# A fused attention and gated-FFN backward kernel: second edge unit turned by DMA in two of four column groups

## The chip, the cores and the metric

The kernel runs on one core of a Trainium2 chip. Its engines work side by side, each through its own instructions in order: TensorE (PE in the profile, its weight loads PEld), VectorE (DVE), ScalarE (ACT), GpSimd (POOL) and SyncE (SP), whose queue issues most DMAs. They wait for one another through semaphores. The metric is the device time of one execution in microseconds (us); lower is better.

## The reference, cut to what matters

The reference is a forward function and its gradients. Input `x` is 2048 rows of 512. Branch A is attention with 32 heads of 16 over a causal window of 256 rows; branch B is a gated FFN with 1376 columns. A sigmoid gate mixes them:

```python
qkv = (x @ wqkv).reshape(B, S, 3, H, Dh)          # transposed to q, k, v per head
scores = jnp.einsum("bhqd,bhkd->bhqk", q, k) * (Dh ** -0.5)
mask = (i - j >= 0) & (i - j < 256)
p = softmax(where(mask, scores, -1e9))
a = einsum("bhqk,bhkd->bhqd", p, v) @ wo
b = (gate * (gate > 0) * up) @ W_down             # gate = x @ W_gate, up = x @ W_up
out = g * a + (1 - g) * b                         # g = sigmoid((x * gate_w).sum(-1))
```

It returns `out` and the gradients of `A_x`, `A_wqkv`, `A_wo`, `B_W_gate`, `B_W_up`, `B_W_down` and `gate_w`, in bf16.

## The kernel before

The program has three stages. The first computes the FFN's products and gradients (lines 205 to 469). The second, which the change touches, computes attention and its gradients (lines 471 to 1089). The third forms the output and the gradient of `x` (lines 1091 to 1180).

**Blocks, units and turns of the loop.** Rows are cut into 16 blocks of 128 (`NT`). Heads are taken in four column groups `c` of eight heads (`DC` is 4). With a window of 256, query block `qb` meets key blocks `qb`, `qb-1` and `qb-2`; the last is the edge, of which only a corner counts. A `Unit` is two heads with up to two blocks. Two units, `x` = 0 and 1, share a loop turn (`turns_`, lines 679 to 702), and share its tiles. For every pair of query blocks there are six loop turns, `k` = 0 to 5: pair turns at 0, 1, 3 and 4, and edge turns at 2 and 5. The last pair of blocks of a group has four turns; the third of them holds a diagonal block with an edge block and counts as edge. A group has 46 turns, the loop 184.

**What one loop turn does** (`while`, line 969). `products` puts the score products S of this turn's units, and the products D of the previous turn's units, on PE. `front` takes the exponential of S into a tile PP (ScalarE, line 746); `mask` zeroes what lies outside the window (GpSimd, line 756); `gradp` multiplies the previous turn's PP by its D into PP's second half (VectorE, line 763). Then every unit's PP, eight blocks of 128 by 128, is needed in two ways:

- As it is, by the sums of the rows (`rowsum`, lines 780 and 782, four small matmuls a call). A row's twelve sums close it; small operations on GpSimd over the next four turns follow. `some_sums` runs at most `quota[0]` of them in a turn, five while the loop has units.
- Turned (transposed), by `cd_piece` (lines 495 and 498), which adds up the gradients of keys and values. It may use a row three loop turns after that row closed, and runs two or three pieces a turn.

**How a unit is turned** (`flip`, line 806). If `u.dma` is set, SyncE issues a DMA transpose of the whole unit, 256 KB (line 809), in the loop turn after the unit's own, when `gradp` is done. Otherwise PE transposes the eight blocks into PSUM two loop turns after the unit's own (line 817) and `share` evicts them on VectorE or ScalarE, whichever its running estimate finds less busy. Before the change `u.dma` holds for unit `x == 0` of every turn with two blocks (but for the very first turns and the very last).

**Tiles.** PP of pair turns has four buffers, PP of edge turns (tag `PPm`) two. Turned tiles of pair units (tag `P2`, line 795) have 14 buffers; those of both edge units share a tile with tag `m`, of four.

**Background work.** Projections of the next rows and groups (`project_parts`), the weight gradients of the group before (`grad_parts`, which read `dar` rows loaded by DMA) and the rest of the FFN's gradients stand in a list `bg`, with a price each. The loop spends them evenly up to the loop turn `until`. When list and jobs are empty in the last group, `early_group` is made: its loads for the third stage (`early`, lines 870 to 873) go out one each turn.

**Third stage.** It works through eight groups of 256 rows. Each group's operands are loaded one group ahead by `load_group`, among them a DMA transpose of `dqkvo_d` (line 912).

Of the kernel before, what the change touches and what calls it, by code (L numbers as in the profile page):

```python
# [11 lines left out]
BF = mybir.dt.bfloat16  # L12
# [10 lines left out]
def kernel(  # L23
# [21 lines left out]
    P = 128  # L45
# [9 lines left out]
    NT = S // P  # L55
    DC = D // P
# [4 lines left out]
    TPG = TGW // P  # L61
# [58 lines left out]
    def wide(name):  # L120
        return wq.tile([P, 2, 2, 4, P], BF, tag="m", bufs=4, name=name)
# [5 lines left out]
    pools = {}  # L127

    def rows_tile(name):
        return st.tile([P, NT, 4, P], BF, tag="rows_st", name=name)  # L130

    if True:
        HH = HG // 2
        proj = {}
        groups = [(c, tg) for c in range(DC) for tg in range(NTG)]
# [69 lines left out]
    with ExitStack() as p1, tc.manual_schedule():  # L205
# [121 lines left out]
        for fc in range(FC):  # L327
            for tg in range(NTG):
                k = Step()
# [141 lines left out]
    if True:  # L471
        p3b = ExitStack()
        pjs["b"] = p3b.enter_context(tc.tile_pool(name="pj", bufs=2))
        wk = p3b.enter_context(tc.tile_pool(name="attw", bufs=2))
# [4 lines left out]
        P2 = {}  # L479
# [26 lines left out]
        def spill(c, t0):  # L506
            tsl = slice(t0, t0 + NT // 4)
            eng = nc.gpsimd if (c == DC - 1 and t0 >= NT // 2) else nc.sync
            eng.dma_start(dqkvo_d[t0 * P:(t0 + NT // 4) * P, c * 4 * P:(c + 1) * 4 * P].rearrange("(t p) n -> p t n", p=P),
                          sts[c][:, tsl, :, :].rearrange("p t a n -> p t (a n)"))  # L510
# [169 lines left out]
        for c in range(DC):  # L680
            def pair_of(q):
                return [(q, q), (q + 1, q)]

            def edges_of(r):
                return [(k, k - 2) for k in (r, r + 1) if 2 <= k < NT]

            for q in range(0, NT, 2):
                if q + 2 < NT:
                    its = ((pair_of(q), 0), (pair_of(q), 2), (edges_of(q + 1), 0), (pair_of(q + 1), 2), (pair_of(q + 1), 0),
                           (edges_of(q + 2), 2))  # L690
                else:
                    its = ((pair_of(q), 0), (pair_of(q), 2), ([(q + 1, q + 1), (q + 1, q - 1)], 0), ([(q + 1, q + 1)], 2))
                for k, (blocks, g) in enumerate(its):
                    two = []
                    for x in range(2):
                        u = Unit()
                        u.c, u.q, u.g, u.x, u.blocks, u.nb, u.at = c, q + k // 3, g + x, x, blocks, len(blocks), len(turns_)
                        u.edge = blocks[-1][1] == blocks[-1][0] - 2
                        u.dma = x == 0 and len(blocks) == 2 and (c > 0 or q > 0 or k >= 3) and (c < DC - 1 or q < NT - 2)
                        u.turn = u.at + (1 if u.dma else 2)  # L700
                        two.append(u)
                    turns_.append(two)
        NI = len(turns_)
# [33 lines left out]
        def flat(t, n):  # L737
            return t.rearrange("p x i r q -> p x (i r q)")[:, :, 0:n]

        def front(us):  # L740
            edge = us[0].edge
            two = wk.tile([P, 2, 2, 4, P], BF, tag="PPm" if edge else "PP", bufs=2 if edge else 4, name="PP")
            for u in us:
                u.two, u.PP = two, two[:, u.x, :, :, :]
            n = 2 * us[0].nb * P
            nc.scalar.activation(two[:].rearrange("p x a b q -> p x a (b q)")[:, :, 0, 0:n], flat(us[0].S[:], n), ACT.Exp)  # L746
# [42 lines left out]
        def place(u):  # L789
            if u.edge:  # L790
                if u.at not in wides:
                    wides[u.at] = wide("p2")
                p2 = wides[u.at][:, u.x if u.nb == 2 else 0, :, :, :]
            elif u.nb == 2 or u.x == 0:
                p2 = pools["p2"].tile([P, 2, 4, P], BF, tag="P2", bufs=14, name="p2")[:]
                wides[u.at] = p2
            else:
                p2 = wides[u.at]
            for i, (qb, kb) in enumerate(u.blocks):
                b = 2 * (i if u.nb == 2 else u.x)  # L800
                P2[(u.c, qb, kb, u.g)] = p2[:, :, b:b + 2, :]
            return p2
# [3 lines left out]
        def flip(u):  # L806
            p2 = place(u)
            if u.dma:
                nc.sync.dma_start_transpose(out=p2.rearrange("p a b q -> p (a b) q"),
                                            in_=u.PP.rearrange("p a b q -> p (a b) q"))  # L810
                return
            if u.nb == 2 or u.x == 0:
                pools["pt"] = ps.tile([P, 2, 4, P], BF, tag="tr", bufs=2, name="pt")
            pt = pools["pt"]
            for a in range(2):
                for b in range(2 * u.nb):
                    nc.tensor.transpose(pt[:, a, b if u.nb == 2 else 2 * u.x + b, :], u.PP[:, a, b, :], ident[:])  # L817
            return (lambda: share(p2, pt[:], 8 * P, True)) if u.nb == 2 or u.x == 1 else None
# [63 lines left out]
        def early_f(i):  # L882
            t = wide("f")[:].rearrange("p u a h q -> p (u a h q)").rearrange("p (k s) -> p k s", s=GT * P)
            gsl = slice(0, GT * P)
            for k0, k1, src in ((8 * i, 8 * i + 8, hT_d), (8 * i - FC, 8 * i + 8 - FC, dgT_d)):
                lo, hi = max(k0, 0), min(k1, FC)
                if lo >= hi:
                    continue
                for k in range(lo, hi):
                    S2.setdefault("f0" if src is hT_d else "f1", []).append(t[:, k - k0, :])  # L890
                full = min(hi, nfull)
                if lo < full:
                    nc.sync.dma_start(t[:, lo - k0:full - k0, :], src[lo * P:full * P, gsl].rearrange("(fc p) s -> p fc s", p=P))
                if hi > nfull:
                    nc.sync.dma_start(t[:, nfull - k0, :], src[F - P:F, gsl])
# [23 lines left out]
        with tc.manual_schedule():  # L919
# [9 lines left out]
            quota = [0]  # L929
            credit = 0.0  # L930
            until = 0
            turn = 0
# [9 lines left out]
            def insert(job):  # L942
                at = 0
                if held:
                    while bg[at][2]:
                        at += 1
                    at += 1
                bg[at:at] = job
# [20 lines left out]
            while turn < NI + 3 or ev or cdq or bg or sums:  # L969
                for e in busy:  # L970
                    busy[e] = max(0.0, busy[e] - 2.3) + (1.0 if e == "act" else 1.25)
                now = ev.pop(turn, [])
                quota[0] = 5 if turn < NI else 99
                us = turns_[turn] if turn < NI else []
                vs = turns_[turn - 1] if 1 <= turn <= NI else []
                for eng, f in now:
# [2 lines left out]
                if us and (turn == 0 or turns_[turn - 1][0].q != us[0].q):  # L979
                    c, j = us[0].c, us[0].q  # L980
                    gi = c * NTG + j // TPG
                    if j == 0:
                        sts[c] = rows_tile("rows_st")
                    if j % TPG == 0:
                        credit = 0.0
                        until = turn + (12 if j < NT - TPG else 10) - ((0 if c > 0 and j >= TPG else 1) if gi + 1 < len(groups) else 6)
                        if j == TPG and c > 0:
                            jobs = ready
                        for _ in range(((2, 1, 0, 0) if c == 0 else (0, 1, 2, 2))[j // TPG]):
                            if jobs:  # L990
                                bg += jobs.pop(0)
                        if gi + 1 < len(groups):
                            insert(project_parts(*groups[gi + 1]) + [(0.0, lambda gi=gi: late.extend(plan.get(gi + 1, [])), False)])
                            if gi + 2 == len(groups):
                                until -= 1
                    if j == 6 and c > 0:
                        for i in range(2):
                            ev.setdefault(turn + 7 + 4 * i, []).append(("dma", lambda c=c - 1, t0=NT // 2 + i * NT // 4: spill(c, t0)))
                    if j == 2 and c > 0:
                        ready = grad_parts(c - 1)  # L1000
                    if c == DC - 1 and j == NT - 2:
                        for i in range(3):
                            ev.setdefault(turn + (5, 6, 8)[i], []).append(("dma", lambda i=i: early_f(i)))
# [4 lines left out]
                if us:  # L1008
                    front(us)
                    mask(us)  # L1010
# [200 lines left out]
```

## Time and profile before

| | |
|---|---|
| three runs | 894.53, 888.96, 895.00 us; median 894.53 |
| profiled execution | 890.63 us, of which the span of its instructions is 888.9 |
| granted TensorE clock, mean | 0.994 |
| attention loop, first exponentials of the groups | 242.3, 349.7, 466.3, 580.5 us; last one at 692.2 |
| PE busy in the span | 848.5 us (95%) |
| VectorE, GpSimd, ScalarE busy | 503.5, 488.5, 387.2 us |
| PE transposes of line 817 | 1512, 115.3 us busy |
| DMA turns of line 809 | 171, median 4.4 us from issue to landing |
| DMA | 161.95 MB; 134, 159, 163 and 192 GB/s in the four groups |

A busy time is the time in which an engine had an instruction in work; on PE the instructions overlap and their ends are modelled, so the mean of one is longer than the step from one to the next. A row of a group of instructions reads: line, engine, operation, output tile <- inputs, count; then busy us and the mean of one in ns; then the engine's idle time before it and what ended that. In a timeline the columns are start, length, engine, line, operation and count, and in brackets the idle time before with its cause. For a DMA the length is the time its issue held the queue of the engine that issued it, not the transfer. A row of waits reads: who <- for whom: us in total, times, the longest.

### The profile page before, as it was taken

What the parts mean: (1) busy time and instruction counts of PE and PEld (TensorE: products, weight loads), DVE (VectorE), ACT (ScalarE), POOL (GpSimd) and SP (SyncE); (2) the same over time, 40 slices, a digit from 0 to 9 for tenths busy, and PEclk for the clock granted to TensorE, in tenths of its full rate; (3) what the DMA queues carried; (4) which work ended last, traced back from release to release, by engine and by line L of the source; (5) the groups of instructions that cost most, each with busy time, mean ns of one, the idle gap of its engine ahead of it and who ended that gap; (6) DMA issues with size and microseconds to landing.
All of it is one profiled execution on the core that took longest, in us unless ns stands there. A gap on an engine that the chain in (4) does not pass through costs nothing. (4 is left out here: it accounts for less than half of the span.)

```text
span 888.9 us, 29258 instructions
## 1 busy us (share of the span) xinstructions
PE 848.5 (95%) x12420; PEld 558.8 (63%) x12545; DVE 503.5 (57%) x755; ACT 387.2 (44%) x561; POOL 488.5 (55%) x900
## 2 busy tenths in 40 slices
PE   7999999999989999989999999999899999999998
PEld 4566556655567877766777767777677744444443
DVE  4445443333277888877778777788777322232222
ACT  5522222232365676755557655667455311111111
POOL 2645445444357778886668776687766532222221
PEclk9999999999999999999999999999999999999999
DMA  9989999999858999999977999899999999777840
GB/s 288 224 194 214 219 218 225 231 216 196 190 79 120 153 146 161 155 143 194 191 120 135 138 220 182 133 168 164 215 202 202 259 211 270 197 193 191 191 116 25
DMA packets 441004, 161.95 MB, mean 182 GB/s; under 512 B 361640, under 2 KB 437640, under 8 KB 440872
## 3 DMA queue, kind: packets, MB, share of 16 engines
q1 hardware_dynamic: 436264, 150.62, 90.2%
q0 software_dynamic: 3024, 8.92, 3.4%
q8 instruction: 98, 1.61, 0.8%
q10 hardware_dynamic: 1584, 0.53, 0.3%
q14 instruction: 34, 0.28, 0.1%
HBM read 38.44 MB, written 38.34 MB: 86 GB/s over the span
## 5 line engine op out<-in xcount | busy, mean ns | idle before, releaser
L763 DVE TENSOR_TENSOR PP<-PP,D 128x1024 bf16<-128x1024 bf16 (+1 forms) x184 | 219.6, 1193 | 72.1 <-POOL PP L756 28.1
L746 ACT ACTIVATE PP<-S 128x1024 bf16<-128x1024 f32 (+1 forms) x184 | 185.2, 1007 | 101.8 <-PE D L713 52.1
L756 POOL TENSOR_SCALAR_AFFINE_SELECT PP<-PP 128x512 bf16<-128x512 bf16 (+1 forms) x188 | 143.9, 767 | 93.4 <-ACT PP L746 92.8
L74 DVE COPY p<-pt 128x1024 bf16<-128x1024 bf16 x167 | 114.4, 685 | 15.5 <-PE pt L817 15.3
L357 POOL TENSOR_TENSOR hgu<-rg,upm 128x512 bf16<-128x512 bf16 x44 | 50.8, 1155 | 119.9 <-DVE upm L355 103.4
L817 PE MATMUL pt<-ident,PP 128*128 128x128 bf16 x1512 | 115.3, 220 | 0.2 <-issue 0.2
L780 PE MATMUL BA<-KV,PP 128*128 128x33 bf16 x1440 | 106.5, 180 | 3.4 <-ACT BAs L72 2.6
L780 PEld LDWEIGHTS <-PP 128*128 128x128 bf16 x1440 | 85.6, 96 | 30.6 <-issue 11.2
L782 PE MATMUL BA<-KV,PP 128*128 128x17 bf16 x1440 | 102.1, 170 | 0.0
L397 PE MATMUL wps<-hgu_r,x_r 128*128 128x256 bf16 x640 | 96.0, 273 | 0.7
L495 PE MATMUL CD<-rq,p 128*128 128x32 bf16 x1440 | 95.0, 177 | 0.0
L498 PE MATMUL CD<-rq,p 128*128 128x16 bf16 x1440 | 93.7, 169 | 0.0
L782 PEld LDWEIGHTS <-PP 128*128 128x128 bf16 x1440 | 84.7, 96 | 9.0 <-issue 4.5
L817 PEld LDWEIGHTS <-PP 128*128 128x128 bf16 x1512 | 87.0, 98 | 0.4 <-issue 0.4
L713 PE MATMUL S<-zT,K 32*128 32x128 bf16 (+3 forms) x1056 | 78.2, 240 | 6.6 <-ACT PP L746 2.9
L495 PEld LDWEIGHTS <-p 128*128 128x128 bf16 x1440 | 80.8, 96 | 0.3
L498 PEld LDWEIGHTS <-p 128*128 128x128 bf16 x1440 | 80.6, 96 | 0.3
L397 PEld LDWEIGHTS <-x_r 128*128 128x128 bf16 x640 | 62.6, 98 | 28.6
L713 PE MATMUL D<-zT,V 32*128 32x128 bf16 (+3 forms) x1056 | 73.1, 239 | 6.5 <-DVE PP L763 5.9
L355 DVE SCALAR_TENSOR_TENSOR upm<-rg,ups 128x512 bf16<-128x512 bf16 x44 | 30.3, 689 | 78.7 <-PE ups L342 55.7
L1123 ACT COPY a_sb<-aps 128x512 f32<-128x512 f32 x16 | 9.4, 586 | 145.0 <-issue 133.1
L365 POOL TENSOR_TENSOR hgu<-dh_sb,rg 128x512 bf16<-128x512 bf16 x44 | 58.7, 1335 | 9.0 <-ACT dh_sb L363 9.0
(145 smaller groups left out, 1485.2 us busy)
## 6 DMA issues: line engine op xcount, KB each, us to landing
hgu_d<-hgu SPq DMA_DIRECT2D x44, 384.0 KB, 3.3
dqkvo_d<-rows_st SPq DMA_DIRECT2D x14, 512.0 KB, 4.6
duT_g<-hgu_d SPq DMA_DIRECT2D x8, 640.0 KB, 6.1
dgT_g<-hgu_d SPq DMA_DIRECT2D x7, 640.0 KB
gt<-hgu_d SPq DMA_DIRECT2D x7, 640.0 KB, 5.9
dar<-da_d SPq DMA_DIRECT2D x16, 256.0 KB, 4.9
dar<-da_d POOLq DMA_DIRECT2D x12, 256.0 KB, 5.0
p<-PP SPq DMA_TRANSPOSE x171, 4.4
```

Source lines behind the costliest of these rows:

```text
L74: nc.vector.tensor_copy(out, in_)
L365: nc.gpsimd.tensor_tensor(out=k.hgu[:, 2, :], in0=dh_sb[:], in1=k.rg[:], op=ALU.mult)
L397: nc.tensor.matmul(acc["w"][:, c, :], lhsT=x_r[:, t, c * P:(c + 1) * P], rhs=k.dgu_r[:, :, i, :], start=(go_ and c % 2 == 0), stop=no_, sk ...
L495: nc.tensor.matmul(cd[0][:, h, :], lhsT=p2[:, 0, pr, :], rhs=rq[:, h, 0:2 * Dh], start=cd[1], stop=True, skip_group_check=True)
L498: nc.tensor.matmul(cd[0][:, h, 0:Dh], lhsT=p2[:, 1, pr, :], rhs=rq[:, h, 2 * Dh:3 * Dh], start=False, stop=True, skip_group_check=True)
L713: nc.tensor.matmul(dst, lhsT=proj[(u.c, kb // TPG)][nm + ("", "1")[par]][rows[par], (kb % TPG) * P:(kb % TPG + 1) * P], rhs=proj[(u.c, qb ...
L746: nc.scalar.activation(two[:].rearrange("p x a b q -> p x a (b q)")[:, :, 0, 0:n], flat(us[0].S[:], n), ACT.Exp)
L756: nc.gpsimd.affine_select(out=out, in_=out, compare_op=ALU.is_ge, fill=0.0, base=0 if up else -1, pattern=[[0, 2], [0, b1 - b0], [1 if up ...
L763: nc.vector.tensor_tensor(out=v(1), in0=v(0), in1=flat(vs[0].D[:], n), op=ALU.mult)
L780: nc.tensor.matmul(BA[:, h, 0:33], lhsT=u.PP[:, 0, 2 * i + pr, :], rhs=kv[:, kb % TPG, h, 1:34], start=(first and pr == 0), stop=True, ski ...
L782: nc.tensor.matmul(BA[:, h, 33:50], lhsT=u.PP[:, 1, 2 * i + pr, :], rhs=kv[:, kb % TPG, h, 0:17], start=False, stop=True, skip_group_check ...
L817: nc.tensor.transpose(pt[:, a, b if u.nb == 2 else 2 * u.x + b, :], u.PP[:, a, b, :], ident[:])
```

## The change

In groups 1 and 2 (the second and third) the second unit of an edge turn gets `u.dma` too, so both halves of that turn are turned by DMA, one loop turn after their own, and PE's transposes and the eviction for it fall away. The edge PP tile has three buffers for two, the turned tile of pair units 12 for 14 (one PP tile is 4 KB in a partition, one turned tile 2 KB, so the memory is the same). At most four sums run in a loop turn, for five, in all groups. In the last row group of the last column group the background list's deadline is three loop turns later.

```diff
@@ -696,7 +696,7 @@
                         u.edge = blocks[-1][1] == blocks[-1][0] - 2
-                        u.dma = x == 0 and len(blocks) == 2 and (c > 0 or q > 0 or k >= 3) and (c < DC - 1 or q < NT - 2)
+                        u.dma = (x == 0 or c in (1, 2) and u.edge) and len(blocks) == 2 and (c > 0 or q > 0 or k >= 3) and (c < DC - 1 or q < NT - 2)
                         u.turn = u.at + (1 if u.dma else 2)
@@ -739,7 +739,7 @@
-            two = wk.tile([P, 2, 2, 4, P], BF, tag="PPm" if edge else "PP", bufs=2 if edge else 4, name="PP")
+            two = wk.tile([P, 2, 2, 4, P], BF, tag="PPm" if edge else "PP", bufs=3 if edge else 4, name="PP")
@@ -792,7 +792,7 @@
-                p2 = pools["p2"].tile([P, 2, 4, P], BF, tag="P2", bufs=14, name="p2")[:]
+                p2 = pools["p2"].tile([P, 2, 4, P], BF, tag="P2", bufs=12, name="p2")[:]
@@ -970,7 +970,7 @@
-                quota[0] = 5 if turn < NI else 99
+                quota[0] = 4 if turn < NI else 99
@@ -983,7 +983,7 @@
-                        until = turn + (12 if j < NT - TPG else 10) - ((0 if c > 0 and j >= TPG else 1) if gi + 1 < len(groups) else 6)
+                        until = turn + (12 if j < NT - TPG else 10) - ((0 if c > 0 and j >= TPG else 1) if gi + 1 < len(groups) else 3)
```

## The prediction, made before the result was known

> **What bounds the kernel now.** I read the page first. Its chain of waits reaches back only to 645 us, but from there it is almost all TensorE, and TensorE is busy in nine tenths of nearly every slice. The change acts on the second and third column groups. Their first exponentials start at 349.7 and 466.3 us and the fourth group's at 580.5 us, so I asked for busy times in those two stretches (columns: stretch, its length, then PE, PE's weight loads, VectorE, ScalarE and GpSimd busy with their counts, granted clock, DMA share, GB/s):
>
> ```profile
> 350.00:466.00 116.00, 108.37 (x2484) 82.23 (x2499) 89.46 (x126) 71.19 (x99) 85.10 (x189) 0.99 1.00 159
> 466.00:580.00 114.00, 107.86 (x2491) 81.88 (x2504) 89.01 (x124) 71.29 (x100) 84.50 (x187) 1.00 0.97 163
> ```
>
> PE is busy 93 to 95% and no other engine passes 79%. Next the waits of PE, first over the two stretches together, then (last two lines) over the whole run; columns are total us, times, longest:
>
> ```profile
> PE D L713 <- DVE PP L763: 2.8, 8, 0.5
> PE pp L150 <- ACT ws L72: 1.8, 2, 0.9
> PE BA L780 <- ACT BAs L72: 1.5, 6, 0.3
> PE wps L605 <- DMA dar<-da_d: 1.4, 1, 1.4
> ...
> PE pp L150 <- DVE p L74: 0.7, 2, 0.4
> ```
> ```profile
> PE D L713 <- DVE PP L763: 5.9, 16, 0.6
> PE S L713 <- ACT PP L746: 2.9, 10, 0.4
> ```
>
> The named waits of the two groups come to 10.2 us in 230. None is for a turned tile. So the order of work on PE sets the pace, and work taken off PE should shorten these groups until something else is late. What could be late is SyncE's queue, which issues every DMA turn. The turns of line 809 in the second group, and a crowded piece of the third:
>
> ```profile
> L809 SPq DMA_TRANSPOSE p<-PP x45: 1231/1284/3557, 350.1 to 464.5; - x45
> ...
> DMA to landing us min/median/max: 3.0/4.4/7.4
> ```
> ```profile
> 516.07 1.99 SPq L809 DMA_TRANSPOSE p<-PP  x1
> 518.16 0.54 SPq L509 DMA_DIRECT2D dqkvo_d<-rows_st  x1
> 518.79 5.91 SPq L809 DMA_TRANSPOSE p<-PP  x3
> ```
>
> One turn holds SyncE for 1.23 us at best (min/median/max in ns), and four in a row beside an HBM store took 7.90 us, 1.98 each. Adding up all issue durations on SyncE's timeline: second group 84.1 us of 116.5 (45 turns with a mean of 1.45, other DMAs 18.9), third 86.1 of 114.2 (44 at 1.53, others 18.8).
>
> **The turns moved to DMA.** A group has 13 edge turns of the loop with two blocks and one mixed turn that counts as edge, so 28 units in two groups leave PE. Each is eight transposes:
>
> ```profile
> 566.44 0.61 PE L817 MATMUL pt<-ident,PP 128*128 128x128 bf16 x8
> 566.88 0.39 PE L188 MATMUL ptp<-ident,V 128*128 128x128 bf16 x4
> ...
> 567.95 0.23 PE L713 MATMUL D<-zT,V 16*128 16x128 bf16 x2 [0.31 <-DVE PP L763]
> ...
> 568.90 0.61 PE L817 MATMUL pt<-ident,PP 128*128 128x128 bf16 x8
> 569.35 0.98 PE L602 MATMUL wps<-rows_st,x_r 128*128 128x384 bf16 x5
> ```
>
> The next work starts 0.44 and 0.45 us after the first of eight. 28 x 0.45 = 12.6 us off PE. They leave turns k=1 and k=4 of each six, whose exponentials are 2.9 and 2.6 us apart; the shortest turns of the trace are 1.5 us, so the chain exponential, mask, product doesn't bind there. I count all 12.6.
>
> With them go 28 evictions of turned tiles (line 74, 685 ns; 85 of the 93 in the two groups are on VectorE). VectorE is busy 78% and PE waited 0.7 us for these copies: 0 to 0.7, I take 0.5 off.
>
> Added: 28 DMA turns on SyncE, each behind the first unit's turn, waiting for the same VectorE product, so no new wait on an engine. Queued behind them are the next turns, the `rows` turn and the `dar` loads. A turned edge tile is first read, by the planner's rule (the row closes, then three turns of the loop), five turns of the loop or more after its issue, some 12 us, against a landing of at most 7.4. So the latency is hidden; what counts is the queue's load. Issue time at the groups' own means: second 59 x 1.45 + 18.9 = 104.5 us, third 58 x 1.53 + 18.8 = 107.5. PE would want 116.5 - 6.3 = 110.2 and 114.2 - 6.3 = 107.9. SyncE goes from three quarters full to level with PE. At the 1.23 minimum it would need 92 and 90 us and cost nothing; at 1.98 a turn 136 and 134. I take +4 us, nearer to the first end: the group means are measured over 100 us, the 1.98 over eight, and queued turns run without the gaps that SyncE now spends waiting for VectorE. The `dar` load that PE once waited 1.4 us for moves behind more turns: 0 to +3, I take +1.
>
> [...]
>
> **Four sums a turn.** A sum is four small matmuls, about 0.11 us by the same timeline (two from 566.02 to 566.24). A row has twelve; five, five, two becomes four, four, four, and the row closes in the same turn. So 0.11 us leaves each of the four pair turns and 0.22 enters each edge turn. In all four groups the edge turns are the short ones (1.5 to 2.3 us) and most of PE's waits for the product and the exponential lie at their ends, as at 567.95. Bounds: nothing, or all of 5.9 + 2.9 = 8.8 us. 26 waits x 0.22 = 5.7 if each is in an edge turn and long enough; I take -4. Should PE be held by SyncE, this gain is lost in the two middle groups.
>
> **Tiles.** Three edge tiles remove no wait of the trace (no exponential waits for a DMA or for PE's last reader); they cover later landings: 0. Eight pair tiles are made every six turns and live about nine, so twelve just do: a DMA turn on SyncE can now wait for the CD matmuls of the same loop turn, about half a microsecond, two turns of six. Behind it stand the other DMAs; PE needs them five turns later, and a late SyncE finds the tile free. 0 to +2; I take 0.
>
> **The last group's deadline** moves by three turns of the loop. PE is full there either way, so spreading saves at most the 0.5 us of waits at 683 to 687. But the loads for the last stage start only when the background list is empty, three turns or some 7 us later:
>
> ```profile
> 680.42 0.53 SPq L870 DMA_DIRECT2D early<-da_d  x1
> ...
> 690.84 9.16 SPq L873 DMA_TRANSPOSE early<-dqkvo_d  x4
> 700.04 1.09 SPq L559 DMA_DIRECT2D wo_z<-in_A_wo_dram  x2
> ```
>
> SyncE works without a gap from 682 to 725; the turn of line 912 at its end lands at 736.1 and PE needs it at 737.8. SyncE had some 5 us free before 690, so the delay that stays is between 0 and 7 us less 1.7 of slack: 0 to +5.3. Most of the queue was already waiting behind the last turns, so I take +1.5.
>
> Sum: -12.6 - 0.5 + 4 + 1 - 4 + 0 + 1.5 = -10.6. The profiled execution took 890.6 us (span 888.9), so 880. The three runs lie between 889.0 and 895.0 with a median of 894.5, 3.9 above it; I place the new median half that far above, 882.
>
> **Rivals.** *SyncE becomes the bound.* The two groups then last 37.7 + 117 x f, f the mean issue of a turn. For: f rose from 1.45 to 1.53 to 1.58 over the groups as their traffic rose from 159 to 192 GB/s, and the third would reach about 200. Against: in the present trace SyncE mostly waits for VectorE (49 us and more in the two groups), and queued turns away from HBM traffic ran at 1.3 to 1.4. At f = 1.65 they last 230.8, as now, and only the first and fourth groups' sums gain: about 890 to 892, no change.
>
> *The same with a loss.* The point is f = 1.67: above it the turned tiles come later than PE did them, and PE's CD matmuls (line 495) wait for landings. At f = 1.8 the groups last 248.3, +17.6, less 3 for the sums: about 905 + 2 = 907, slower.
>
> *PE isn't the limit.* Weight loads cover only 82 of 116 us. If those, not the matmul bars, tell PE's load, a quarter of PE is free, the transposes lie in that room, and only the sums' 4 us come: 889. Against it stand the 10 us of named waits in 230. [...]
>
> *The last stage starts late.* All else as forecast, but line 912's turn is the full 5.3 us late: about 886.
>
> **Chances.** Forecast 0.54; SyncE as bound without loss 0.18; PE not the limit 0.08; late last stage 0.06; SyncE with loss 0.14. About 1%, 9 us here, is what a measurement can tell from no change, so faster is under 885.6 and slower over 903.5: 0.54, 0.32, 0.14. The forecast's own range is 871 (all 8.8 us of the sums and no SyncE cost: 890.6 - 12.6 - 8.8 + 2) to 885. For eight in ten the range reaches up through the no-change cases to f = 1.75 (37.7 + 204.8 = 242.5, +11.8, less 4): 898 + 2 = 900.
>
> **What would show it.** Right: the two groups last 109 to 112 and 107 to 111 us; line 817 has 1288 matmuls and line 809 199 turns; the waits for the product and the exponential fall by about half in all groups; no PE wait at line 495. Wrong: line 809's mean issue above 1.67 us with PE waiting at line 495 for landings, or ScalarE waiting for a tile at line 746; a wait of PE for line 912's turn near 735 us; or groups that stay at 116 and 114 us with PE's busy share fallen.

## The result and the profile after

The changed kernel took 905.91 us (median of six runs, 898.12 to 913.60); the kernel before, beside it, 894.76 (six runs, 888.96 to 902.74). The ratio is 1.0116, with a 95% interval of 1.0068 to 1.0163: about 1.2% slower, where 1.5% faster was forecast and 900 was the range's upper end. The ratio is taken over the faster runs alone; the run of 913.60 us is not in it. The profiled execution took 903.35 us, 12.7 more than the one of before, with a span of 901.3 and a mean granted clock of 0.982 (0.994 before).

First the stretches of the second and third groups of the changed kernel, with the columns that the prediction explained:

```profile
348.00:466.00 118.00, 105.59 (x2403) 77.47 (x2420) 82.73 (x117) 69.86 (x98) 85.78 (x191) 0.96 1.13 181
466.00:587.00 121.00, 106.90 (x2391) 78.03 (x2410) 81.81 (x113) 70.20 (x98) 85.16 (x188) 0.93 1.16 179
```

The transposes are gone: PE has some 80 to 100 fewer recorded matmuls in each. But the groups became longer, from 116.5 and 114.2 us to 117.7 and 120.9 between first exponentials, and PE's busy share fell from 93 to 95% to 88 to 89%. The clock column fell too. The fourth group, to the end of its last exponential, went from 112.3 to 114.7 us, the first from 107.4 to 105.8, and what follows the last exponential from 196.1 to 199.9.

The waits from 348 to 600 us, the two groups and the first 13 us of the fourth, in order of size (total us, times, longest):

```profile
...
ACT PP L746 <- DMA p<-PP: 13.7, 5, 4.2
...
PE BA L780 <- ACT BAs L72: 9.5, 7, 4.5
...
PE pp L150 <- ACT ws L72: 3.7, 2, 3.0
```

The first row doesn't exist before: there the exponential never waits for a DMA. Now it does, for the tile PP that it is to write, which a DMA turn is still reading. All five waits are at pair turns of the loop; one of them, 2.6 us, lies in the fourth group. The second row was 1.5 us with a longest of 0.3, and stands among PE's own waits: PE waits for a copy by ScalarE (`BAs`, line 72), which has nothing to do with DMA. It stands behind that exponential in ScalarE's order.

One such place, on three engines. SyncE's queue (start, duration, queue, line, operation, count):

```profile
554.25 5.17 SPq L809 DMA_TRANSPOSE p<-PP  x3
559.51 0.53 SPq L509 DMA_DIRECT2D dqkvo_d<-rows_st  x1
560.09 1.83 SPq L526 DMA_TRANSPOSE p<-in_A_wqkv_dram  x1
562.01 0.58 SPq L589 DMA_DIRECT2D out_dram<-ws  x1
562.70 3.86 SPq L809 DMA_TRANSPOSE p<-PP  x2
```

ScalarE at that time (idle time before it and what ended it, in brackets), then PE:

```profile
562.50 0.59 ACT L72 CAST K<-pp 128x512 bf16<-128x512 f32 x1 [0.91 <-PE pt L817]
567.27 1.02 ACT L746 ACTIVATE PP<-S 128x1024 bf16<-128x1024 f32 x1 [4.18 <-DMA p<-PP]
568.19 0.49 ACT L72 COPY BAs<-BA 128x400 f32<-128x400 f32 x1
```
```profile
563.80 0.39 PE L188 MATMUL ptp<-ident,K 128*128 128x128 bf16 x4
568.73 0.19 PE L780 MATMUL BA<-KV,PP 128*128 128x33 bf16 x1 [4.54 <-ACT BAs L72]
```

SyncE issues without a pause. Turns queue up behind a 512 KB store and two other transfers, so the turns of old PP tiles go out late. ScalarE needs one of those tiles back and stands for 4.18 us; the copy behind it is late by as much; PE stands for 4.54 us. From the end of a product to the issue of its turn, the delay was 0.6 us on average in both groups before (longest 3.0) and is 4.8 and 5.2 us now (longest 9.8 and 11.8). The turns of line 809 in the third group (duration of an issue in ns, minimum/median/maximum; then time to landing):

```profile
L809 SPq DMA_TRANSPOSE p<-PP x57: 1231/1351/4141, 465.9 to 584.6; - x57
...
DMA to landing us min/median/max: 3.1/4.6/8.9
```

The median issue is still near the shortest, the longest is 4.1 us, and the mean over all of SyncE's turns in that group is 1.66 (1.53 before). All issues on SyncE add up to 104.9 us of 117.7 in the second group and 114.2 of 120.9 in the third (84.1 and 86.1 before).

**What the time is made of.** Over the loop, from the first exponential to the last, the profiled run lost 8.6 us (450.5 to 459.1), and behind it 3.8. I added up PE's records in the loop. Idle stretches longer than 0.7 us rose from 4.9 to 19.3 us (+14.4). All the rest, PE at work with its short gaps, fell from 445.7 to 439.7 (-6.0), not by the 12.6 forecast. Part of what is missing is the clock. The trace grants either 1.0 or 0.5, in stretches of 3.4 us or twice that, and half-clock stretches in the loop rose from 10.2 to 30.7 us. Two neighbouring windows of the changed kernel, around the stall above:

```profile
556.00:565.00 9.00, 7.93 (x174) 5.82 (x174) 6.87 (x10) 4.72 (x7) 5.53 (x12) 1.00 1.18 156
565.00:573.00 8.00, 4.05 (x78) 2.34 (x79) 1.63 (x3) 3.68 (x6) 3.42 (x10) 0.57 1.24 189
```

The clock (third column from the end) is 1.00 until the stall and 0.57 on average after it. Of the six half-clock stretches in the loop, five begin 1.5 to 4.3 us after the start of a PE stall of 1.35 to 4.54 us. The sixth, at 490.6 us, follows two waits of only 0.42 and 0.51 us, and a stall of 1.83 us at 646.5 us has none behind it. Comparing the step from one matmul to the next in these stretches with the steps of the same lines at full clock in the kernel before, the work in them took some 21 to 22 us where it would have taken 14 to 16: about 6.5 us more, against some 2.5 in the kernel before. That is a rough estimate from one run each.

### The profile page after: what moved, and what is told of

The parts are those of the page before. It is cut to its first block, busy times and chain, and to the rows that moved or that the text cites. A ratio compares the mean times of both kernels' runs of the same rounds, so it can differ in the third digit from the quotient of the medians.

```text
span 901.3 us, 28805 instructions
## 1 busy us (share of the span) xinstructions
PE 842.3 (93%) x12191; PEld 548.2 (61%) x12321; DVE 487.9 (54%) x732; ACT 383.2 (43%) x556; POOL 488.3 (54%) x900
## 5 line engine op out<-in xcount | busy, mean ns | idle before, releaser
L780 PEld LDWEIGHTS <-PP 128*128 128x128 bf16 x1440 | 86.2, 96 | 32.4 <-issue 14.1
L74 DVE COPY p<-pt 128x1024 bf16<-128x1024 bf16 x143 | 97.8, 684 | 6.6 <-PE pt L817 6.5
L817 PE MATMUL pt<-ident,PP 128*128 128x128 bf16 x1288 | 98.1, 220 | 0.1
L782 PEld LDWEIGHTS <-PP 128*128 128x128 bf16 x1440 | 85.1, 97 | 17.8 <-issue 13.9
L713 PE MATMUL S<-zT,K 32*128 32x128 bf16 (+3 forms) x1056 | 80.2, 242 | 8.0 <-ACT PP L746 3.4
L817 PEld LDWEIGHTS <-PP 128*128 128x128 bf16 x1288 | 74.3, 98 | 0.2 <-issue 0.2
```

The costliest lines, as they stand in the source:

```text
L74: nc.vector.tensor_copy(out, in_)
L713: nc.tensor.matmul(dst, lhsT=proj[(u.c, kb // TPG)][nm + ("", "1")[par]][rows[par], (kb % TPG) * P:(kb % TPG + 1) * P], rhs=proj[(u.c, qb ...
L780: nc.tensor.matmul(BA[:, h, 0:33], lhsT=u.PP[:, 0, 2 * i + pr, :], rhs=kv[:, kb % TPG, h, 1:34], start=(first and pr == 0), stop=True, ski ...
L782: nc.tensor.matmul(BA[:, h, 33:50], lhsT=u.PP[:, 1, 2 * i + pr, :], rhs=kv[:, kb % TPG, h, 0:17], start=False, stop=True, skip_group_check ...
```

## The experiments

The ratios are against runs of the kernel before on the same chip.

**1. The condition alone** (`e_dma_only`), put into the kernel before:

```diff
-  u.dma = x == 0 and len(blocks) == 2 and ...
+  u.dma = (x == 0 or c in (1, 2) and u.edge) and len(blocks) == 2 and ...
```

> The kernel before with the changed condition for u.dma alone (two edge PP tiles, 14 turned pair tiles, five sums, old deadline). Theory A (the 28 further turns overload SyncE's queue; pair PP tiles come free late, ScalarE waits for landings, TensorE stalls and its clock is halved for 3.4 us windows): slower than before by 0.5 to 2%, some 895 to 910 us, mean issue of a turn above 1.55 us in groups 1 and 2, ScalarE waiting for DMA at line 746. Theory B (twelve turned tiles make SyncE wait for TensorE and so hold up its queue; the turns by themselves are fine): faster than before by about 1%, 880 to 887 us, lags of the turns below 5 us.

Measured: 906.91 us, ratio 1.0161 (1.0084 to 1.0238). The middle groups last 119.9 and 117.9 us, ScalarE waits 22.8 us in the run for DMA turns. The condition by itself makes the whole loss; the other four edits neither cause it nor cure it.

**2. The other edits without the condition** (`e_no_dma`): the changed kernel with the old condition, so twelve `P2` tiles, three edge tiles, four sums, the later deadline.

> The changed kernel without the changed condition (twelve turned tiles, three edge PP tiles, four sums, later deadline stay). Theory A: no slower than before, 885 to 892 us, the sums' gain of 0 to 4 us kept. Theory B: most of the loss stays, 897 to 906 us, with SyncE waiting for TensorE at line 809 and lags of several us.

Measured: 893.80 us, ratio 1.0024 (0.9981 to 1.0066). So the fewer turned tiles aren't the loss. In the profiled run the loop is 4.5 us shorter (446.0), but it starts 2.0 us later and what follows it is 3.6 longer (199.7): in sum nothing is gained.

**3. Four sums alone** (`e_q4_only`), in the kernel before:

```diff
-  quota[0] = 5 if turn < NI else 99
+  quota[0] = 4 if turn < NI else 99
```

> The kernel before with four sums a turn in place of five, nothing else. Theory A: 0 to 5 us faster than before (the first group of the changed kernel, which has no further DMA turns, is 1.6 us shorter than before). A theory that the later sums hold PP tiles longer and so cost time: slower by 2 us or more.

Measured: 893.82 us, ratio 1.0010 (0.9965 to 1.0054). A gain of 4 us, or 0.45%, lies outside this interval. Its profiled loop is 1.7 us shorter and its tail 2.3 longer.

**4. The 28 units not turned at all** (`e_skip`): the kernel before, with the second edge units of the two groups neither transposed on PE nor by DMA; the gradients of keys and values read the first unit's half in their place, so every other instruction stays.

> The kernel before in which the 28 second edge units of groups 1 and 2 are not turned at all, neither by TensorE nor by DMA; the CD matmuls read the first unit's turned half in their place, so the gradients of keys and values are not the reference's for those heads. It measures what TensorE's saving is worth without the queue's load. If TensorE sets the pace: 10 to 13 us faster than before, 879 to 884 us, groups 1 and 2 at 108 to 111 us. If TensorE is not the limit: at most 4 us faster.

Measured: 881.93 us, ratio 0.9868 (0.9812 to 0.9924). Its two groups:

```profile
349.00:459.00 110.00, 103.25 (x2398) 76.78 (x2413) 82.02 (x115) 70.36 (x98) 85.34 (x191) 1.00 1.06 168
459.00:568.50 109.50, 102.70 (x2387) 76.31 (x2407) 80.64 (x111) 70.38 (x99) 84.15 (x188) 1.00 0.98 169
```

With the transposes gone and nothing in their place the groups fall to 109.9 and 109.4 us, and PE is at 94% again. So PE does set the pace of the loop, and this work is worth about 12 us (7 to 17 by the interval). Doing it by DMA, then, costs about 24 (905.9 less 881.9; 22 by the ratios).

**5. A fifth pair tile** (`e_pp5`): the changed kernel with `bufs=2 if edge else 5` in line 742, so that a late turn has one more pair tile before ScalarE needs it back. For the memory, the edge tiles go back from three to two.

> The changed kernel with five pair PP tiles and two edge PP tiles (four and three before; same memory). Theory A, with the reuse of pair PP tiles as the place where the late turns are paid: the waits of ScalarE for DMA at line 746 vanish, 4 to 13 us faster than the changed kernel, 888 to 900 us. If the place is another (the tiles read by the CD matmuls, the dar loads): within 3 us of the changed kernel. Theory B: no faster than the changed kernel.

Measured: 902.55 us, ratio 1.0102 (1.0032 to 1.0172), not to be told from the changed kernel's 1.0116. In its profiled run (917.0 us, the slowest of the four) ScalarE still waits 24.8 us for DMA turns, but seven of the eight waits are now at edge turns of the loop, which have two tiles again. Run 1, with two edge tiles and four pair tiles, has six of its twelve waits there. So this run took a tile from one place and paid there; what five pair and three edge tiles together would do was not tried.

**6. Fewer other issues on SyncE** (`e_relief`): in the changed kernel the `dar` loads, the stores of weight gradients and the spills are issued by GpSimd.

```diff
-                 load_da(i, nc.sync)
+                 load_da(i, nc.gpsimd)
```

> The changed kernel with the dar loads, the stores of weight gradients and the spills of the attention stage issued by GpSimd instead of SyncE, some 7 us of SyncE's issue time per group and no byte of traffic. If it is SyncE's issue time that is short: lags of the turns fall by half and the time by 5 us or more, to 890 to 900 us. If it is the 16 DMA engines that drain too slowly (issues are stretched because of traffic): the mean issue of a turn rises or stays above 1.6 us, groups 1 and 2 stay within 2 us of the changed kernel.

Measured: 915.39 us, ratio 1.0227 (1.0173 to 1.0281): a miss. SyncE's issues in the two groups still add up to 108 and 107 us although it issues fewer, since the mean issue of a turn rose to 1.73 and 1.72. So an issue's length isn't a fixed price: it rose although SyncE had less to issue. But the run doesn't show that SyncE's issue time is no limit, since the issues cost something on GpSimd too. In the loop GpSimd's go from 12 to 54, 9.0 to 40.0 us, and hold up its masks:

```profile
362.95 2.91 POOL L575 DMA_DIRECT2D dar<-da_d  x4
365.88 0.65 POOL L756 TENSOR_SCALAR_AFFINE_SELECT PP<-PP 128x512 bf16<-128x512 bf16 x1
366.56 1.22 DVE L763 TENSOR_TENSOR PP<-PP,D 128x1024 bf16<-128x1024 bf16 x1 [2.49 <-POOL PP L756]
367.83 0.39 PE L713 MATMUL D<-zT,V 16*128 16x256 bf16 x2 [3.23 <-DVE PP L763]
```

Four loads hold GpSimd for 2.91 us, the mask behind them is late, VectorE's product with it, and PE stands for 3.23 us. Over the loop PE's waits for the product are 18.5 us here and 9.0 in the changed kernel, those for `dar` loads 7.0 and 0.4.

**7. Half of the units** (`e_half`): the condition of the change with `k == 2` added, 14 units.

> The kernel before with the changed condition for one of the two edge turns of six only (k = 2), so 14 further DMA turns and 14 units off TensorE. If the loss has a threshold, SyncE's queue being full only at the whole dose: 3 to 6 us faster than before, 887 to 890 us, lags mostly below 5 us, the mean granted clock as before. If the cost is the same for each turn: slower than before by about half of the changed condition's loss, some 899 us.

Measured: 893.94 us, ratio 0.9989 (0.9950 to 1.0028). The second and third groups last 113.4 and 114.3 us and the fourth 118.4; the saving and the cost cancel. ScalarE waits 5.8 us for DMA in the loop, 4.7 of them in the fourth group, although that group has no further turns.

**8. Turns by themselves** (`m_flips`): not the kernel. DMA turns of 256 KB issued back to back on SyncE, alone, then beside twelve 512 KB stores to HBM, then beside twelve 512 KB loads, both issued by ScalarE.

> The disputed cost by itself; nothing of the reference is computed. 24 turns of 128 by 1024 issued by SyncE back to back, then 32 beside HBM stores of 512 KB issued by ScalarE, then 32 beside HBM loads of 512 KB. If the issue alone sets the rate: 1.23 to 1.3 us a turn in all three. If the DMA engines set it: near 1.3 us alone, 1.6 to 2 us beside the stores and the loads.

Measured: alone, and beside the stores:

```profile
L70 SPq DMA_TRANSPOSE dst<-src x25: 1254/1332/1337, 2.5 to 35.6; - x25
...
DMA to landing us min/median/max: 3.2/3.3/3.5
```
```profile
L70 SPq DMA_TRANSPOSE dst<-src x18: 1255/2495/4651, 36.9 to 80.6; - x18
...
DMA to landing us min/median/max: 3.2/5.7/11.0
```

Alone a turn goes out every 1.37 us and lands after 3.3. Beside the stores the sixteen turns from 38.3 us on took 42.3 us in place of 21.9 (16 x 1.37), so each of twelve stores cost the turns 1.7 us; beside the loads it was 42.9, about the same. By these prices (turns at 1.37, other bytes at 512 KB in 1.75 us) the DMA work of the third group is some 84 us of 114 before and 103 of the 108 that PE would want after: from about three quarters to nearly full. This is an estimate.

**9 and 10. The condition in one group only**, in the kernel before: in the first (`e_g0`, `c == 0`, 14 units), where the same account gives some 0.65 before and 0.85 to 0.9 after, and in the third (`e_g2`, `c == 2`, 14 units).

> The kernel before with the second edge units turned by DMA in the first column group alone (13 units). Capacity theory (a turn costs the DMA engines about 1.37 us, other traffic about 1.85 us per 512 KB; a group loses once these fill more than some nine tenths of its time): the first group moves least (134 GB/s) and would be filled to 0.67 before, 0.9 with them, so it gains: 3 to 6 us faster than before, about 889 us, first group at 101 to 104 us. A theory that any second turn behind the first in an edge turn of the loop costs by itself: no gain or a loss, first group at 106 us or more.

> The same in the third column group alone (14 units). Capacity theory: filled to 0.75 before and 0.96 with them, so this group loses its gain: its length 114 to 121 us, the time 892 to 902 us, a lower granted clock there. The other theory: the same change of length as in the first group.

Measured: `e_g0` 897.47 us, ratio 1.0039 (1.0007 to 1.0070); the first group went from 107.4 to 111.4 us, ScalarE waits 9.1 us for DMA turns in three places. That is a miss for the account by averages: by that account a tenth or more of the group's DMA time was free, and it lost all the same. `e_g2`: 902.90 us, ratio 1.0090 (1.0058 to 1.0121), as the account had it; the third group lasts 119.2 us and ScalarE waits 16.4 us. An average fill below one didn't protect the loop: in the first group a turn now goes out 3.5 us after its product on average (0.7 before), the latest 8.6. One rival is untested here: both kernels have two edge tiles, the changed one three, and all three waits of `e_g0` and 11.0 of the 16.4 us of `e_g2` are at edge turns.

**11 and 12. Without the loads of `dar` rows**, in the changed kernel (`e_nodar`) and in the one before (`e_b_nodar`). The output-weight gradient reads rows of `x` in their place, so the matmuls stay and 2 MB of transfers a group are left out; the number of turns isn't touched.

```diff
-                a = gwp.tile([P, 2, D], BF, tag="dar", bufs=4, name="dar")
...
-                    rows[2 * i + e] = a[:, e, :]
-                eng.dma_start(a[:], da_d[...])
+                    rows[2 * i + e] = x_r[:, 2 * i + e, :]
```

> The changed kernel without the dar loads of the attention stage for groups 0 to 2 (16 of 256 KB on SyncE's or GpSimd's queue per two groups); the output weight's gradient of these groups is formed with rows of x in their place, so it is not the reference's. The loads are about 7 us of the DMA engines' time per group, while the number of turns stays. Capacity theory: filled to about 0.9 instead of 0.96, the groups 2 and 3 lose most of their waits: 6 to 15 us faster than the changed kernel, 885 to 898 us. If the number of turns in SyncE's queue is what costs: within 3 us of the changed kernel.

> The kernel before, without the loads of da rows; the output-weight gradient reads rows of x in their place, so 2 MB of transfers a group are left out and every matmul stays. It is the control of the changed kernel without these loads, which took 884.9 us. If the loads cost only where the DMA engines are nearly full (they are at about 0.75 of a group here by the price of 1.37 us a turn and some 1.9 us a 512 KB transfer), this kernel gains little, 889 to 895 us, and the change gains 5 to 10 us over it once the loads are gone. If the loads cost in any kernel, whatever the turns (their waits, their issues on SyncE), it gains as the changed one did, 875 to 882 us, and the change still loses or breaks even without them.

Measured: 884.93 us for the changed kernel, ratio 0.9899 (0.9857 to 0.9942), and 883.50 for the one before, 0.9876 (0.9832 to 0.9920). Without these loads the change makes no difference that can be told; with them it costs 11 us. So most of the net loss comes only with these loads, at the same number of turns. But the control came out against what the account by averages said: the kernel before gained 11 us as well, where 0 to 5 was expected. And the 12 us of PE work still don't show. The waits of the changed kernel without the loads (the lines stand two higher in this file) show where it is lost:

```profile
ACT PP L744 <- DMA p<-PP: 11.5, 7, 2.3
```
```profile
PE BA L778 <- ACT BAs L72: 9.3, 12, 2.7
```

ScalarE still waits for turns, PE behind it, in more and shorter stalls: 10.2 us of PE idle over 0.7 us against 1.5 in the control, and 17.1 us of half clock against 3.4.

**13. Stalls of set length** (`m_clock`): not the kernel, no DMA; 150 to 165 matmuls of 128x512 back to back, then a stall, 28 times. This and the next are for the clock.

> Not the reference's computation: some 150 matmuls of 128x512 back to back, then a stall of PE made by 0 to 8 copies on VectorE (about 0.5 to 5.5 us), and so on 28 times, each stall four times at other places. If a stall of some 1.3 us or more halves the granted clock, as the traces of the kernels suggest, the stalls of up to 1 us leave it at 1.0 and every longer one is followed within 4 us by one window of 3.4 us or more at 0.5. [...] If the half clock in the kernels comes from something else (the DMA load, power), no stall here is followed by it.

Measured: of the twelve stalls of 0.71 to 1.91 us none was followed by a half-clock stretch; of the eight of 2.63 and 3.36 us six were; of the eight of 4.81 and 6.26 us all. The windows around one stall of 2.63 us (the columns are PE, weight loads, VectorE, GpSimd, clock, DMA share, GB/s):

```profile
146.00:152.00 6.00, 3.32 (x16) 1.39 (x15) 2.46 (x5) 0.00 (x0) 1.00 0.00 0
152.00:156.00 4.00, 4.00 (x13) 1.43 (x11) 0.00 (x0) 0.00 (x0) 0.57 0.00 0
```

PE is at work through the whole second window, yet the granted clock is 0.57 on average over its 4.00 us, which is 3.4 us at 0.5, as long as the shorter stretches in the loop. So here a stall of 2.63 us alone brought the half clock, with no DMA (a share of 0.00) and with work waiting. In the loop half-clock stretches also came after stalls of 1.35 us.

**14. Six stalls in the kernel before** (`e_stall`), in loop turns 54, 66, 78, 100, 112 and 124:

```diff
+                if turn in (54, 66, 78, 100, 112, 124):
+                    hold = wk.tile([P, 60], F32, tag="hold", bufs=1, name="hold")
+                    for _ in range(56):
+                        nc.vector.memset(hold[:], 0.0)
```

> The kernel before, with 56 small writes to a scratch tile on VectorE ahead of the product of line 763 at six loop turns of the second and third groups, about 4 us each; no DMA is added. PE should stall for 2 to 3 us at each, 12 to 18 us in all. If the stall halves the clock and the half clock costs time of its own, six windows of 3.4 to 6.8 us at 0.5 show, and the time rises by the stalls and another 1.7 to 3.4 us for each: 22 to 38 us, to 916 to 932 us. If the half clock costs nothing beside the stall, the rise is that of the stalls alone, 12 to 18 us or less, 906 to 912 us, and if no window shows, the half clock of the changed kernel has another cause.

Measured: 959.00 us, ratio 1.0720 (1.0665 to 1.0774). The edit overshot: PE stood for 8.6 to 10.0 us each time, 57.3 in all. With each stall come 10.2 to 13.7 us at half clock (a mean of 0.52 from 370 to 384 us, where VectorE's writes last until 376.8). The time rose by 65.3 us (959.0 less 893.7), 8.0 more than the stalls, 1.3 us for each: less than the 1.7 to 3.4 expected. Work in the loop's half-clock stretches took some 5 to 8 us longer than at full clock by the same rough estimate as above, so in this loop half the clock is far from twice the time. The steps say why: sums of 33 columns go from 25 to 27 ns, transposes of 128 columns from 55 to 107. The stalls cost themselves, 57.3 us, and a smaller part again, 8.0 us, of which that estimate gives the clock 5 to 8.

## Why the prediction was wrong, point by point

**What bounds the kernel, and the -12.6 for the turns.** Right. Leaving the 28 units out gained about 12 us (882 against 894) and PE's busy share stayed at 94%. The rival "PE isn't the limit" falls with it: weight loads cover 70 to 72% of these groups, and yet taking off 12.6 us of PE work shortened them by 11.4.

**SyncE's queue, +4.** This is the step that failed, in its size and its mechanism. It multiplied 59 and 58 turns by the groups' own mean issue and let the queue cost only what its sum would exceed PE's. The means were of a queue with pauses. The mean issue rose to 1.58 and 1.66, and the sums were near the forecast (104.9 and 114.2 for 104.5 and 107.5). But the queue fell behind before it was full (its issues cover 89 and 94% of the groups), by 5 us on average, and the delay is paid wherever somebody needs a tile back. Turning the units by DMA cost about 24 us where +4 and +1 were set down. The runs show what it hangs on: the cost is the condition's alone (1), and half as many units break even (7). Taking away the `dar` loads removes some 9 of the 11 us of net loss (11, 12). Whether SyncE's own issue time or the DMA engines' work holds the queue up in this loop isn't settled (6); that other transfers stretch the issues is shown outside the kernel (8: a median issue of 2.50 us beside the stores, 1.33 alone).

The shortest issue, 1.23 us, was taken as one end. Alone, turns run at 1.37 us each (8), which is 191 GB/s.

**Tiles, 0.** Wrong in its reason. "No exponential waits for a DMA" was a fact of the trace before, and the step took it to hold afterwards. The prediction traced who reads a turned tile, five loop turns later and covered, as it proved: no PE wait at line 495 to speak of (one stop of 1.35 us stands at line 498, with no cause named). It didn't ask who writes over the tile that the turn reads. That is the exponential, in a pair PP tile of which there are four, used again six loop turns later. The third edge tile of the change doesn't touch that, but it does what the prediction said of it, cover later landings: in the changed kernel no wait is at an edge turn, without that tile half of them are (1). A fifth pair tile in its place didn't cure the loss (5). Twelve `P2` tiles cost nothing (2).

**The rival "the same with a loss".** Its result was about right (907, slower; chance 0.14) and its place and condition were not: f never passed 1.67 in the groups, and the wait came at line 746, not line 495. (By its own formula the groups last as before at f = 1.65, not 1.67.) The list of signs named line 746 too. That the rival's number fits is luck.

**Four sums, -4.** The profiled loop without the condition is 4.5 us shorter, but the time isn't (2, 3): with the profile's longer tail nothing is left that can be measured, and a gain of 4 us lies outside both intervals. In the changed kernel PE's waits for the product rose from 5.9 to 9.0 us, where half was expected to go.

**The last group's deadline, +1.5.** What follows the last exponential is 3.6 to 3.8 us longer with all the other edits, with or without the condition, and 2.3 longer with four sums alone. PE waits once for 1.6 us at 735 us, the time named, but for GpSimd and not for line 912's turn. The deadline wasn't tried alone, and with the old deadline the tail varied as much (4.4 us longer in `e_g0`), so +1.5 is neither shown nor excluded. The queue that the step read as without a gap from 682 to 725 us has one of 0.85 us, at 706.

**The clock**, not in the prediction. After 14 of the 16 stalls of 2.63 us or more in (13) it fell to 0.5, and by the rough estimate some 4 of the lost us (6.5 less 2.5) are its part. That such stalls bring the half clock is measured there, and the traces show that the changed kernel has more of both (19.3 us of idle stretches over 0.7 us for 4.9, 30.7 us of half clock for 10.2); its share of the time is an estimate.

**Open.** Why the average account fails in the first group (9), and why the `dar` loads cost the kernel before 11 us as well, though its PE waits name only 1.4 us for them. Part of the second is in the profiles: without the loads the loop is 6.4 us shorter, PE's idle stretches over 0.7 us fall from 4.9 to 1.5 us and half-clock stretches from 10.2 to 3.4. The times also scatter less, 882.8 to 885.0 us against 888.5 to 900.4 beside it. Both may be bursts on the DMA engines, and in the first group the two edge tiles; no run isolates them.

## What to carry to other kernels

When work moves from a full engine to a DMA queue, price it by the queue's free time beside its other traffic, not by one issue; here a group lost 4 us that the averages put at 0.85 to 0.9 full. Then look for who must write over the source of the transfer, not only who reads its result: here ScalarE's wait of 4.18 us for such a tile held up the copy behind it in its order, and PE stood for 4.54 us. A kernel with the work left out altogether tells what the move can bring at most.

## What the runs showed of the hardware

- A DMA transpose of 256 KB from SBUF to SBUF went out every 1.37 us alone; beside 512 KB stores that ScalarE issued, its issue held SyncE for up to 4.65 us and landing took up to 11.0 us (8).
- Amid dense matmuls 14 of 16 PE stalls of 2.6 us or more were followed by 3.4 us or more at half the granted clock, and none of twelve of 1.9 us or less (13). In this loop stalls of 1.35 us were followed by it too, and one of 1.83 us wasn't. Steps of 33-column matmuls hardly change at half clock (25 to 27 ns); those of 128 columns double (55 to 107 ns) (14).
